# Routing two token blocks at a time, one step of the float64 conversion as a product on ScalarE, and one attention bias table with the local keys first

## Chip, cores and metric

One NeuronCore of a Trainium2 chip runs the whole program. The metric is the device time of one execution in microseconds (us), as the median of several runs. The engines are TensorE (PE in the profile; PEld is its weight load), VectorE (DVE), ScalarE (ACT), GpSimd (POOL) and SyncE (SP), which issues all DMAs.

## What is computed

Windowed attention, then a dense layer with a softmax-times-itself activation and layer norm, then soft routing to 32 slots of 8 experts. Cut to what matters:

```python
# attention: B=4, H=8, S=768, D=64; 8 global keys, 96 local ones; ALiBi bias
scores = q @ k.T / sqrt(D) - slopes * dist           # where (global or local), else -1e9
attn_out = softmax(scores) @ v                       # -> x: 3072 tokens x 512
# dense layer (w_in, w_out, g_ln come as float64)
h = x @ w_in                                         # 512 -> 1024
solu = h * softmax(h)
x = (layer_norm(solu) * g_ln) @ w_out                # 1024 -> 512
# routing
logits = x @ phi                                     # 32 slots
slot_input = softmax(logits, over tokens).T @ x
slot_out = relu(slot_input @ w1[e]) @ w2[e]          # per expert, 32 MB of weights
out = softmax(logits, over slots) @ slot_out
```

## The kernel before

The 3072 tokens are 24 blocks of 128. `fast` (line 949) writes the work down block by block: for block t `att_quad` twice (four heads each, line 569), `x_out`, and seven blocks later `later(u)` (line 931), which is `moe(u)` (dense layer, line 654) and `slots_of(u)` (line 735). Nothing is issued in that order: every instruction is first noted by `Plan`, which gives it a time, dependences and a priority (the table `AHEAD` by stage, and `STAY`, a penalty for a change of the array's shape on TensorE) and from these makes one order for all five engines (`order`, line 273), issued at line 297. So nearly every row of the profile has line 297, and groups are told apart by operation, shape and buffers. In these names `b` is a PSUM bank, `s` one of 25 SBUF slots, `small` statistics, `l` the routing logits of a block, `d` their exponentials by token, `w` the 1024x32 routing weights (w_out times phi), `sel` a 0/1 matrix that sums four row groups, `acc` the running slot input, `c_all` the weights by slot.

The stages overlap, in this order. **Start**: the bias tables (`window_tables`, line 441) and the conversion of the float64 weights in 16 pieces of 128x512 (`from_f64`, line 492) beside the first attention blocks. Without a float64 unit a piece is converted in integers: ScalarE scales the low word (line 502), VectorE cuts out and shifts the exponent and the high mantissa in four instructions (503 to 506), GpSimd adds both (508); for w_in ScalarE then rounds and GpSimd makes the remainder (515, 516).

```python
502  nc.scalar.mul(out=r, in_=lo.bitcast(U32), mul=2.0 ** -29)
503  v.tensor_scalar(out=e, in0=hi, scalar1=0x7FFFFFFF, scalar2=None, op0=ALU.bitwise_and)
504  v.tensor_scalar(out=f32v(e), in0=f32v(e), scalar1=2.0 ** -15, scalar2=None, op0=ALU.max)
505  v.tensor_scalar(out=e, in0=e, scalar1=3, scalar2=0x3FFFFFF8, op0=ALU.logical_shift_left, op1=ALU.bitwise_and)
506  v.scalar_tensor_tensor(out=a, in0=hi, scalar=-0x40000000, in1=e, op0=ALU.bitwise_and, op1=ALU.bitwise_or)
```

**Middle**: attention, dense layer and routing of all blocks, interleaved. TensorE uses its array in four shapes (rows by columns): 128x128 for the dense layer, transposes and the sums with `sel`; 64x128 for scores; 128x64 for probabilities times v; 128x32, four side by side, for `w` times the transposed block (writes 32x128) and for `d` times the block (32x256). `slots_of(u)` transposes the block z into `zt`, multiplies by `w`, copies the logits to `l`, sums them with `sel` by slot and by token, takes maxima on VectorE, exponentials on ScalarE, transposes back, copies to `d`, multiplies with z and adds to `acc`. The banks, `l` and `d` are one set, so blocks follow each other.

**End**: the last block's chain, then the expert weights (`in_wx_dram`, 32 loads of 1 MB on SP's queue, in a slot as soon as it is free), and the output.

Of the kernel before, what the change touches and what calls it, by code (L numbers as in the profile page):

```python
# [19 lines left out]
P = 128  # L20
# [37 lines left out]
class Plan:  # L58
# [10 lines left out]
    TURN, STAY, DEEP = 68, 1405, 240  # L69
    WRITES = ("out", "accum_out")  # L70
    AHEAD = {"att": -306, "conv": -240509, "ct": -76279, "down0": 1160935, "down1": 247683, "init": -225381, "load": -1194339, "logits": -93870, "moe": -2182, "out0": 754080, "out1": 854704, "slots": -134, "sums": -1633483, "tab": 1280994, "tail": -566822, "up": -455794, "w": -331203, "w2": -130175}
# [57 lines left out]
    def time(self, eng, method, args):  # L129
# [10 lines left out]
        if eng == "ACT":  # L140
            more = 93 * hasattr(args.get("bias"), "tensor") + 105 * ("accum_out" in args)
            return (52 if psum else 94) + n * 0.833 + more
        if method == "tensor_tensor":
            return 70 + n * (2.5 if self.cols(args["in1"]) == 512 else 1.87)
# [128 lines left out]
    def order(self, rounds=6, look=102):  # L273
# [46 lines left out]
class Build:  # L320


    def __init__(self, tc, nc, a, out, mem):
# [8 lines left out]
        self.rt_st = Ring(st[:, 104 + 4 * i:108 + 4 * i] for i in range(3))  # L332
# [108 lines left out]
    def window_tables(self):  # L441


        self.stage("tab", 0)
        nc = self.nc
        n = WIN + NGMAX
        win, first = self.tabs[False], self.tabs[True]
        rel, key, keep, nd, past, near = (self.part(S_ZX, n * i, n) for i in range(6))
        ri, ki = (self.part(S_ZX, n * (6 + i), n).bitcast(I32) for i in range(2))
        big = int(BIGF)  # L450
        for tl, o, m, step, base, ch in (
            (ri, 0, PREV, -1, PREV, 1), (ri, PREV, NGMAX, 0, big, 0), (ri, WIN - P, P, -1, 0, 1), (ri, WIN, NGMAX, -1, 0, 1),
            (ki, 0, PREV, 0, big, 0), (ki, PREV, NGMAX, 1, 0, 0), (ki, WIN - P, P, 0, big, 0), (ki, WIN, NGMAX, 1, 0, 0),
        ):
            nc.gpsimd.iota(tl[:, o:o + m], pattern=[[step, m]], base=base, channel_multiplier=ch)
# [36 lines left out]
    def from_f64(self, name, rows, cols, out):  # L492


        nc, v, g = self.nc, self.nc.vector, self.nc.gpsimd
# [73 lines left out]
    def att_quad(self, t, hq):  # L569
# [4 lines left out]
        o, n = (WIN - P, P) if first else (0, WIN)  # L574
        m = WIN - P
# [16 lines left out]
        for i2 in range(2):  # L592
            q = i2 * QK
            with self.together():
                for i, (a, b) in enumerate(parts):
                    for j in range(2):
                        r = slice(64 * j, 64 * j + 64)
                        nc.tensor.matmul(out=ps[j][:, 256 * i2:256 * i2 + n], lhsT=a[r, q:q + P], rhs=b[r, q + P + o:q + QK],
                                         start=(i == 0), stop=(i == len(parts) - 1))
        for h in range(4):  # L600
            i2, j = divmod(h, 2)
            nc.vector.tensor_tensor_reduce(
                out=pr[:, h, o:], in0=ps[j][:, 256 * i2:256 * i2 + n], in1=self.tabs[first][:, 4 * hq + h, :], scale=-0.125,
                scalar=3.0e38, op0=ALU.add, op1=ALU.min, accum_out=st[:, h:h + 1],
            )
        for h in range(4):
            nc.scalar.activation(out=pr[:, h, o:], in_=pr[:, h, o:], func=AF.Exp, bias=st[:, h:h + 1], scale=-1.0,
# [5 lines left out]
        for i2 in range(2):  # L613
            w = pr[:, 2 * i2:2 * i2 + 2]
            nc.gpsimd.tensor_tensor(out=w[:, :, o:], in0=w[:, :, o:],
                                    in1=share[:, 2 * i2:2 * i2 + 2].unsqueeze(2).to_broadcast([P, 2, WIN - o]), op=ALU.mult)
# [3 lines left out]
            with self.together():  # L620
                for j in range(2):
                    nc.tensor.transpose(pt[:, j, :], w[:, j, m:], self.ident)
                if not first:
                    for j in range(2):
                        nc.tensor.transpose(pt[0:m, 2 + j, :], w[:, j, 0:m], self.ident)
# [84 lines left out]
    def last_logits(self, shift, scale):  # L710
# [16 lines left out]
        l4 = self.l4_ring()[0]  # L727
# [7 lines left out]
    def slots_of(self, u):  # L735
        self.stage("slots", u)
        nc = self.nc
        z = self.z.pop(u)
        if u == self.last:
            l4, dT, d = self.l4_ring()  # L740
            by_slot, by_token, pd = self.bank(ZT)[:, 0:P], l4[:, 0:NS], self.bank(LD)
            nc.tensor.transpose(by_slot, l4, self.ident)
        else:
            zt = self.zt_ring().rearrange("p (c n) -> p c n", c=8)
            for half in range(2):
                ps = self.bank(ZT)
                with self.together():
                    for c in range(4):
                        o = (half * 4 + c) * P
                        nc.tensor.transpose(ps[:, c * P:(c + 1) * P], z[:, o:o + P], self.ident)  # L750
                nc.scalar.copy(out=zt[:, half * 4:half * 4 + 4, :], in_=ps.rearrange("p (c n) -> p c n", c=4))
            pl = pd = self.ld_bank(u)
# [463 lines left out]
```

## Time and profile before

| | us |
|---|---|
| runs of before | 442.66, 442.77, 444.25 (median 442.77) |
| the profiled execution, whole | 441.79 |
| its span, first to last instruction | 439.9 |
| TensorE busy | 404.5 (92%) |
| VectorE, ScalarE, GpSimd busy | 335.4, 304.1, 189.2 |
| mean granted TensorE clock | 0.987 |

The span and the 1.9 us around it make the profiled execution's 441.79. TensorE is busy over nine tenths of the span, but the share is an average over stages with different limits, so the stages are read one by one below.

### The profile page before, as it was taken

Reading aid. Unit: us, or ns where it says so; the run is one execution under the profiler, and the core shown is the slowest. Engines: PE = TensorE matmul, PEld = TensorE weight load, DVE = VectorE, ACT = ScalarE, POOL = GpSimd, SP = SyncE. Lnnn points to the kernel's source line nnn. Section 1 sums busy time; section 2 is a strip of 40 time slices with the busy share of each in tenths; the row PEclk is TensorE's granted clock in tenths of the full one; section 3 lists DMA queues with packets and bytes.
Section 4 is the critical chain, followed back from the end, with each engine's and each line's share of the span. In section 5 each row is a group of like instructions: output and inputs, shape, how many; then the busy total and the mean of one; then the engine's idle time right before and its main releaser. Section 6 shows DMA issues by size and latency. Waiting matters only on the chain.

```text
span 439.9 us, 10437 instructions
## 1 busy us (share of the span) xinstructions
PE 404.5 (92%) x3617; PEld 294.4 (67%) x3617; DVE 335.4 (76%) x1337; ACT 304.1 (69%) x973; POOL 189.2 (43%) x181
## 2 busy tenths in 40 slices
PE   2898978999999999999999999999999999899960
PEld 1465655787777887877878778778777776424540
DVE  7878898999997889887778777888768799401370
ACT  4789888876688888988898778988646546411240
POOL 1488887666345365755465465555100003300000
PEclk9999999999999999999999999999999999999995
DMA  7957574636130413233124213202702599899597
GB/s 285 320 199 252 179 250 169 237 99 227 78 115 17 180 35 115 94 116 113 44 79 163 82 74 115 92 2 98 288 20 92 190 369 373 326 397 419 223 338 229
DMA packets 20140, 78.02 MB, mean 177 GB/s; under 512 B 2480, under 2 KB 8624, under 8 KB 15984
## 3 DMA queue, kind: packets, MB, share of 16 engines
q1 hardware_dynamic: 20080, 77.28, 48.7%
q8 instruction: 30, 0.49, 0.5%
q14 instruction: 30, 0.25, 0.2%
HBM read 70.98 MB, written 6.29 MB: 176 GB/s over the span
## 4 chain that ended last, share of the span: by engine, by line
PE 75%; POOL 8%; DVE 6%; ACT 3%; issue 2%; DMA 2%; POOLq 0%; DVEq 0%; ACTq 0%
PE b L297 75%; POOL s L297 8%; ACT s L297 3%; DVE s L297 3%; DVE small L297 2%; DMA out_dram<-s 1%; DMA small<-in_n_dram 1%; DVE acc L297 0%; DVE l L297 0%; ACT l L297 0%; ACT c_all L297 0%; DVE d L297 0%; POOLq L297 0%; DVE sel L297 0%; DVE c_all L297 0%
## 5 line engine op out<-in xcount | busy, mean ns | idle before, releaser
L297 PE MATMUL b<-s,s 128*128 128x512 f32 (+3 forms) x1568 | 235.3, 348 | 6.5 <-ACT s L297 2.8
L297 PEld LDWEIGHTS b<-s,s 128*128 128x128 f32 (+3 forms) x1568 | 150.0, 153 | 52.5 <-issue 14.6
L297 ACT COPY s<-b 128x256 f32<-128x256 f32 (+2 forms) x244 | 95.1, 436 | 46.2 <-PE b L297 44.5
L297 ACT ACTIVATE s<-s,small 128x240 f32<-128x240 f32 (+2 forms) x215 | 117.3, 552 | 10.8 <-DVE small L297 10.8
L297 POOL TENSOR_TENSOR s<-s,small 128x480 f32<-128x480 f32 (+1 forms) x96 | 92.4, 982 | 73.4 <-DVE small L297 50.8
L297 POOL TENSOR_TENSOR s<-s,s 128x736 fp32r<-128x736 f32 (+2 forms) x56 | 89.6, 1603 | 55.1 <-DVE s L297 19.4
L297 PE MATMUL b<-ident,s 128*128 128x128 f32 (+1 forms) x600 | 92.1, 280 | 3.4 <-ACT s L297 2.0
L297 PEld LDWEIGHTS b<-ident,s 128*128 128x128 f32 (+1 forms) x600 | 68.9, 141 | 27.1 <-issue 10.3
L297 DVE CUSTOM_DVE_ANT_0 s<-b,s 128x240 f32<-128x240 f32 (+1 forms) x192 | 65.3, 379 | 6.5 <-PE b L297 5.6
L297 DVE TENSOR_SCALAR small<-small 128x1 f32<-128x1 f32 (+1 forms) x322 | 61.5, 216 | 7.0 <-ACT s L297 2.9
L297 PE MATMUL b<-s 64*128 64x240 f32 (+2 forms) x528 | 52.4, 322 | 9.5 <-DMA s<-in_qkv_dram 6.6
L297 PEld LDWEIGHTS b<-s 64*128 64x128 f32 (+1 forms) x528 | 39.0, 195 | 22.4 <-issue 7.7
L297 DVE TENSOR_REDUCE small<-b 128x1 f32<-128x128 f32 (+2 forms) x95 | 42.3, 463 | 11.9 <-PE b L297 9.3
L297 ACT ACTIVATE s<-b,small 128x512 f32<-128x512 f32 x49 | 33.5, 690 | 16.6 <-DVE small L297 15.2
L297 ACT ACTIVATION_READ_ACCUMULATOR s<-s,small 128x1 f32 x215 | 42.4, 197 | 0.0
L297 DVE SCALAR_TENSOR_TENSOR s<-b,s 128x512 f32<-128x512 f32 x48 | 31.9, 686 | 3.8 <-ACT s L297 3.5
L297 DVE TENSOR_SCALAR s<-s 128x512 int32<-128x512 int32 (+2 forms) x51 | 32.3, 665 | 2.6 <-ACT s L297 2.5
L297 DVE COPY s<-b 128x512 f32<-128x512 f32 (+1 forms) x20 | 12.3, 635 | 23.6 <-PE b L297 22.9
L297 POOL CAST s<-c_all 128x256 fp32r<-128x256 f32 x6 | 2.4, 396 | 60.1 <-DVE s L297 53.6
L297 ACT CAST s<-b 128x512 fp32r<-128x512 f32 (+1 forms) x32 | 18.3, 570 | 14.3 <-PE b L297 14.3
L297 DVE TENSOR_SCALAR s<-s,small 128x1024 f32<-128x1024 f32 (+1 forms) x25 | 23.8, 951 | 0.3
L297 ACT CAST s<-s 128x736 fp32r<-128x736 f32 (+2 forms) x26 | 18.6, 720 | 5.3 <-PE b L297 2.5
(86 smaller groups left out, 315.8 us busy)
## 6 DMA issues: line engine op xcount, KB each, us to landing
s<-in_wx_dram SPq DMA_DIRECT2D x32, 1024.0 KB, 7.8
s<-in_qkv_dram SPq DMA_DIRECT2D x24, 992.0 KB, 4.9
out_dram<-s SPq DMA_DIRECT2D x12, 512.0 KB, 5.5
s<-in_v_tail_dram SPq DMA_DIRECT2D x20, 224.0 KB, 5.6
s<-in_w_in_dram SPq DMA_DIRECT2D x8, 512.0 KB, 6.7
s<-in_w_out_dram SPq DMA_DIRECT2D x8, 512.0 KB, 3.8
acc<-in_phi_dram SPq DMA_DIRECT2D x1, 64.0 KB, 10.2
small<-in_n_dram SPq DMA_DIRECT2D x1, 2.0 KB, 2.7
```

The lines of the kernel that those rows point to most:

```text
L297: f(*(self.now(x, age) for x in a), **{k: self.now(x, age) for k, x in kw.items()})
```

## The change

Four things, and a new order. (1) `later` calls `slots_of(u - 1, u)` after every odd block up to 21; blocks 22 and 23 go alone. For a pair the sum by slot is one matmul of 256 columns, the logits copy, the maxima, the exponentials by slot, the copy to `d` and the update of `acc` are done once, the exponentials by token twice; the eight `d` matmuls follow each other and add up in PSUM. `l` and `d` share one buffer; `zt` has two, the second in slot S_TAB + 1. (2) In `from_f64` ScalarE multiplies the high word, read as a float, by 2^-112; VectorE keeps a shift and the merge. (3) One bias table of 256 columns per head, with the keys of the block itself first, serves first and other blocks. The host lays out keys and values to match, so the same number of DMAs loads them. (4) The planner's numbers (`AHEAD`, `STAY`, `look`, two costs) are others. What is computed is the same.

```diff
-    TURN, STAY, DEEP = 68, 1405, 240
+    TURN, STAY, DEEP = 68, 1362, 240
...
-    AHEAD = {"att": -306, "conv": -240509, "ct": -76279, ...
+    AHEAD = {"att": -720, "conv": -1209974, "ct": 295072, ...
...
-        for hp in range(4):
-            for h in (2 * hp, 2 * hp + 1):
-                for dst, o, m in ((win, 0, WIN), (first, WIN, NGMAX)):
-                    nc.vector.scalar_tensor_tensor(
-                        out=dst[:, h, 0:m], in0=nd[:, o:o + m], scalar=8.0 * SLOPES[h], in1=keep[:, o:o + m],
-                        op0=ALU.mult, op1=ALU.add,
-                    )
-            hs = slice(2 * hp, 2 * hp + 2)
-            nc.scalar.copy(out=first[:, hs, NGMAX:], in_=win[:, hs, WIN - P + NGMAX:])
+        for h in range(H):
+            nc.vector.scalar_tensor_tensor(out=self.table[:, h, :], in0=nd, scalar=8.0 * SLOPES[h], in1=keep, op0=ALU.mult,
+                                           op1=ALU.add)
...
         nc.scalar.mul(out=r, in_=lo.bitcast(U32), mul=2.0 ** -29)
-        v.tensor_scalar(out=e, in0=hi, scalar1=0x7FFFFFFF, scalar2=None, op0=ALU.bitwise_and)
-        v.tensor_scalar(out=f32v(e), in0=f32v(e), scalar1=2.0 ** -15, scalar2=None, op0=ALU.max)
-        v.tensor_scalar(out=e, in0=e, scalar1=3, scalar2=0x3FFFFFF8, op0=ALU.logical_shift_left, op1=ALU.bitwise_and)
-        v.scalar_tensor_tensor(out=a, in0=hi, scalar=-0x40000000, in1=e, op0=ALU.bitwise_and, op1=ALU.bitwise_or)
+        nc.scalar.mul(out=f32v(e), in_=f32v(hi), mul=2.0 ** -112)
+        v.tensor_scalar(out=e, in0=e, scalar1=3, scalar2=None, op0=ALU.logical_shift_left)
+        v.scalar_tensor_tensor(out=a, in0=hi, scalar=-0x80000000, in1=e, op0=ALU.bitwise_and, op1=ALU.bitwise_or)
...
+            nc.vector.tensor_copy(out=l4, in_=pl[:, 0:k * P])
...
+                nc.tensor.matmul(out=by_slot, lhsT=self.sel4, rhs=l4, start=True, stop=True)
+                for i in range(k):
+                    nc.tensor.matmul(out=by_token[:, i, :], lhsT=l4[:, i * P:(i + 1) * P], rhs=self.sel4[:, 0:32], start=True,
+                                     stop=True)
...
+        nc.vector.tensor_copy(out=d, in_=pd[:, 256:256 + k * P].rearrange("p (k n) -> p k n", k=k)[:, :, 0:NS])
+        with self.together():
+            for i, z in enumerate(zs):
+                for fq in range(4):
+                    nc.tensor.matmul(out=pd[32 * fq:32 * fq + 32, 0:256], lhsT=d[:, i, :], rhs=z[:, fq * 256:(fq + 1) * 256],
+                                     start=(i == 0), stop=(i == k - 1), tile_position=(0, 32 * fq))
...
         self.moe(u)
-        self.slots_of(u)
+        if u == self.last - 1 or u == self.last:
+            self.slots_of(u)
+        elif u % 2:
+            self.slots_of(u - 1, u)
...
-        self.zt_ring = Ring([self.part(S_ZX, 1024, 1024)])
+        self.zt_ring = Ring([self.part(S_ZX, 1024, 1024), self.part(S_TAB + 1, 0, 1024)])
```

Three places show how the order moves. First, TensorE in the middle: `b_68` is the routing bank, `b_61` to `b_67` the others, `w_72` or `w_71` the routing weights. Before, the four `d` matmuls of one block and the eight `w` matmuls of a later one:

```order
L297 MATMUL b_68<-s_100,d 32x256 x4
L297 MATMUL b_66<-s_96,s_92 128x512
L297 MATMUL b_65<-s_94,s_92 128x512
L297 MATMUL b_66<-s_94,s_92 128x512
L297 MATMUL b_63<-ident,s_84 128x128 x2
L297 MATMUL b_63<-ident,s_84 112x128 x2
L297 MATMUL b_67<-ident,s_84 128x128 x2
L297 MATMUL b_67<-ident,s_84 112x128 x2
L297 MATMUL b_68<-s_101,w_72 32x128 x8
```

Now, those of two pairs:

```order
L297 MATMUL b_67<-ident,s_98 128x128 x4
L297 MATMUL b_68<-s_99,l_69 32x256 x8
L297 MATMUL b_64<-s_1118,s_87 64x128 x2
L297 MATMUL b_64<-s_1118,s_84 64x128 x2
L297 MATMUL b_67<-ident,s_98 128x128 x4
L297 MATMUL b_66<-s_93,s_91 128x512
L297 MATMUL b_68<-s_82,w_71 32x128 x8
L297 MATMUL b_68<-s_100,w_71 32x128 x8
```

Eight `d` and sixteen `w` matmuls now stand together, so the shape 128x32 is entered half as often for them.

Second, ScalarE at the start. `s_103`, `s_104` are conversion buffers before and `s_101` to `s_103` now, with `s_104`, `s_105` the raw float64 data; `s_84` or `s_83` hold attention probabilities. Before:

```order
L297 CAST s_101<-s_101 128x256 x2
L297 COPY s_83<-s_82 128x2x112 x3
L297 ACTIVATE s_84,small<-s_84,small 128x128 x4
L297 COPY s_83<-s_82 128x2x112
L297 ACTIVATE s_103<-s_105 128x512
L297 ACTIVATE s_84,small<-s_84,small 128x128 x4
L297 ACTIVATE s_104<-s_105 128x512
```

Now:

```order
L297 CAST s_100<-s_100 128x256 x2
L297 ACTIVATE s_101<-s_104 128x512
L297 ACTIVATE s_102<-s_104 128x512
L297 ACTIVATE s_101<-s_104 128x512
L297 ACTIVATE s_103<-s_104 128x512
L297 ACTIVATE s_83,small<-s_83,small 128x128 x4
L297 ACTIVATE s_102<-s_105 128x512
L297 ACTIVATE s_103<-s_105 128x512
```

Two pieces of the conversion now come ahead of the first exponentials, and the four table copies are gone. On SP's queue the first two pieces of w_in now stand ahead of the first block's `in_qkv_dram` load, which was first.

Third, VectorE after the last block's dense layer, whose bn_stats and bn_aggr mark the place (`s_100` or `s_99` is the last z). Before:

```order
L297 SCALAR_TENSOR_TENSOR s_100,small<-b_61,s_101 128x512
L297 COPY d<-b_68 128x32
L297 COPY l_69<-b_63 128x128
L297 SCALAR_TENSOR_TENSOR s_100,small<-b_62,s_101 128x512
L297 SCALAR_TENSOR_TENSOR acc<-acc,small,b_68 128x256
L297 BN_STATS small<-s_100 128x6
L297 TENSOR_REDUCE small<-b_63 128x1
L297 TENSOR_REDUCE small<-small 128x2
L297 TENSOR_SCALAR small<-small 128x1 x2
L297 BN_STATS small<-s_100 128x6
L297 TENSOR_SCALAR small<-small 128x1
L297 BN_AGGR small<-small 128x2
```

Now:

```order
L297 SCALAR_TENSOR_TENSOR acc<-acc,small,b_68 128x256
L297 SCALAR_TENSOR_TENSOR s_99,small<-b_61,s_100 128x512
L297 SCALAR_TENSOR_TENSOR s_99,small<-b_62,s_100 128x512
L297 BN_STATS small<-s_99 128x6
L297 COPY l_69<-b_68 128x128
L297 BN_STATS small<-s_99 128x6
L297 TENSOR_REDUCE small<-small 128x2
L297 TENSOR_SCALAR small<-small 128x1 x2
L297 TENSOR_REDUCE small<-b_68 128x1
L297 TENSOR_SCALAR small<-small 128x1
L297 BN_AGGR small<-small 128x2
```

Blocks 20 and 21 are now done as one ahead of this place, so fewer routing instructions of earlier blocks stand between those of the last block.

## Rows read from the trace of the kernel before

**Rows 1.** Windows by stage: us; then busy us (instructions) of each engine; clock, DMA.

```profile
20.00:77.00 57.00, 49.51 (x401) 31.88 (x401) 49.01 (x166) 49.54 (x167) 47.48 (x42) 1.00 0.62 211
77.00:364.00 287.00, 286.81 (x2550) 224.87 (x2547) 242.30 (x1012) 222.40 (x716) 129.34 (x107) 1.00 0.34 122
364.00:379.00 15.00, 13.32 (x137) 8.59 (x135) 13.66 (x61) 9.05 (x32) 5.57 (x10) 1.00 0.94 380
```

**Rows 2.** Timeline of PE in the middle: start, us, operation, count.

```profile
203.87 0.64 PE L297 MATMUL b<-s,d 128*32 128x256 f32 x8
204.44 0.73 PE L297 MATMUL b<-s,s 128*128 128x512 f32 x2
205.01 1.04 PE L297 MATMUL b<-ident,s 128*128 128x128 f32 x8
205.98 0.94 PE L297 MATMUL b<-s 64*128 64x240 f32 x12
206.85 0.66 PE L297 MATMUL b<-ident,s 128*128 128x128 f32 x4
207.43 0.32 PE L297 MATMUL b<-s,w 128*32 128x128 f32 x4
```

**Rows 3.** Timeline of PE in windows of 0.01 to 0.05 us, for single starts.

```profile
205.45 0.49 PE L297 MATMUL b<-ident,s 128*128 128x128 f32 x3
...
204.78 0.39 PE L297 MATMUL b<-s,s 128*128 128x512 f32 x1
...
200.30 0.63 PE L297 MATMUL b<-s,s 128*128 128x512 f32 x2
...
200.53 0.63 PE L297 MATMUL b<-s,s 128*128 128x512 f32 x2
```

**Rows 4.** Groups by line and form, 20 to 77 us: count, busy us, mean ns, idle before.

```profile
L297 DVE TENSOR_SCALAR s<-s 128x512 int32<-128x512 int32 x16 | 13.5, 853 | 0.0
...
L297 DVE TENSOR_SCALAR s<-s 128x512 f32<-128x512 f32 x8 | 6.3, 783 | 0.0
L297 ACT ACTIVATE s<-s 128x512 int32<-128x512 uint32 x9 | 6.1, 682 | 0.3 <-POOL s L297 0.3
```

**Rows 5.** Timeline of DVE and POOL near 18 us, and of DVE near 23 us.

```profile
18.07 1.27 POOL L297 TENSOR_TENSOR s<-s,s 128x512 int32<-128x512 int32 x1 [2.56 <-DVE s L297]
...
18.11 1.52 DVE L297 TENSOR_SCALAR s<-s 128x512 int32<-128x512 int32 x1
...
22.93 0.42 DVE L297 TENSOR_SCALAR s<-s 128x512 int32<-128x512 int32 x1
```

**Rows 6.** Groups by line and form, whole span.

```profile
L297 DVE SCALAR_TENSOR_TENSOR acc<-acc,small,b 128x256 f32<-128x256 f32 x23 | 11.0, 476 | 4.3 <-PE b L297 4.0
...
L297 DVE COPY l<-b 128x128 f32<-128x128 f32 x24 | 6.9, 287 | 6.1 <-PE b L297 5.8
L297 DVE TENSOR_REDUCE small<-b 128x1 f32<-128x128 f32 x24 | 6.9, 286 | 3.6 <-PE b L297 3.3
...
L297 DVE COPY d<-b 128x32 f32<-128x32 f32 x24 | 4.6, 190 | 4.9 <-PE b L297 4.6
...
L297 DVE TENSOR_REDUCE small<-b 128x1 f32<-128x32 f32 x23 | 4.3, 187 | 1.8 <-ACT l L297 1.6
...
L297 ACT COPY s<-s 128x224 f32<-128x224 f32 x4 | 1.5, 374 | 5.6 <-DVE s L297 5.6
```

**Rows 7.** Chain that ended last, 365.8 to 378.2 us: shares, then pieces (start, us).

```profile
by line: DVE small L297 48.3%; DVE acc L297 14.5%; DVE s L297 11.7%; PE b L297 8.2%; ACT s L297 5.5%; DVE l L297 4.3%; DVE d L297 3.8%; ACT l L297 3.6%; issue 3.0%; DVE c_all L297 2.2%; DVEq L297 0.6%
...
368.09 2.38 DVE small L297 x12
...
377.56 0.40 DVE acc L297
```

**Rows 8.** Waits of the whole span: who for whom, us, times, longest.

```profile
PE b L297 <- DMA s<-in_qkv_dram: 6.6, 1, 6.6
...
PEld b L297 <- DMA s<-in_wx_dram: 0.3, 1, 0.3
```

More of the change, by code (lines that the diff above doesn't have):

```diff
@@ L271, in schedule, with order @@
         return start, fin, nth
-    def order(self, rounds=6, look=102):
+    def order(self, rounds=6, look=121):
         n = len(self.ops)
@@ L331, in __init__ @@
         self.ln_st = Ring(st[:, 48 + 14 * i:62 + 14 * i] for i in range(4))
-        self.rt_st = Ring(st[:, 104 + 4 * i:108 + 4 * i] for i in range(3))
+        self.rt_st = Ring(st[:, 104 + 6 * i:110 + 6 * i] for i in range(2))
         self.rs_st = Ring(st[:, 116 + 2 * i:118 + 2 * i] for i in range(4))
@@ L573, in att_quad @@
         first = t % NQB == 0
-        o, n = (WIN - P, P) if first else (0, WIN)
-        m = WIN - P
+        n, m = P if first else WIN, WIN - P
         x = self.qkv[t]
@@ L597, in att_quad @@
                         r = slice(64 * j, 64 * j + 64)
-                        nc.tensor.matmul(out=ps[j][:, 256 * i2:256 * i2 + n], lhsT=a[r, q:q + P], rhs=b[r, q + P + o:q + QK],
+                        nc.tensor.matmul(out=ps[j][:, 256 * i2:256 * i2 + n], lhsT=a[r, q:q + P], rhs=b[r, q + P:q + P + n],
                                          start=(i == 0), stop=(i == len(parts) - 1))
@@ L602, in att_quad @@
             nc.vector.tensor_tensor_reduce(
-                out=pr[:, h, o:], in0=ps[j][:, 256 * i2:256 * i2 + n], in1=self.tabs[first][:, 4 * hq + h, :], scale=-0.125,
+                out=pr[:, h, 0:n], in0=ps[j][:, 256 * i2:256 * i2 + n], in1=self.tabs[first][:, 4 * hq + h, :], scale=-0.125,
                 scalar=3.0e38, op0=ALU.add, op1=ALU.min, accum_out=st[:, h:h + 1],
@@ L732, in last_logits, with slots_of @@
         )
-    def slots_of(self, u):
-        self.stage("slots", u)
+    def slots_of(self, *us):
+        self.stage("slots", us[0])
         nc = self.nc
[L738 to L741, printed above, removed]
+        k = len(us)
+        zs = [self.z.pop(u) for u in us]
+        l4_all = self.l4_ring()
+        l4, dT = (l4_all[:, 0:P], l4_all[:, P:]) if us[0] == self.last else [l4_all[:, 0:k * P]] * 2
+        d = l4_all[:, 0:k * NS].rearrange("p (k s) -> p k s", k=k)
+        if us[0] == self.last:
+            pd, by_slot, by_token = self.bank(LD), self.bank(ZT)[:, 0:P], l4[:, 0:NS].unsqueeze(1)
@@ L752, in slots_of @@
-            pl = pd = self.ld_bank(u)
-            by_slot, by_token = pl[:, 128:256], pl[:, 256:288]
-            with self.together():
-                for r in range(2):
-                    for g in range(4):
-                        nc.tensor.matmul(out=pl[32 * g:32 * g + 32, 0:P], lhsT=self.w2[:, r * 4 + g, :],
-                                         rhs=zt[:, r * 4 + g, :], start=(r == 0), stop=(r == 1), tile_position=(0, 32 * g))
-            l4, dT, d = self.l4_ring()
-            nc.vector.tensor_copy(out=l4, in_=pl[:, 0:P])
@@ L761, in slots_of @@
-            nc.tensor.matmul(out=by_slot, lhsT=self.sel4, rhs=l4, start=True, stop=True)
-            nc.tensor.matmul(out=by_token, lhsT=l4, rhs=self.sel4[:, 0:32], start=True, stop=True)
+            pl = pd = self.ld_bank(us[0])
+            by_slot, by_token = pl[:, 256:256 + k * P], pl[:, 0:k * NS].rearrange("p (k s) -> p k s", k=k)
+            for i, z in enumerate(zs):
+                zt = self.zt_ring().rearrange("p (c n) -> p c n", c=8)
+                for half in range(2):
+                    ps = self.bank(ZT)
+                    with self.together():
+                        for c in range(4):
+                            o = (half * 4 + c) * P
+                            nc.tensor.transpose(ps[:, c * P:(c + 1) * P], z[:, o:o + P], self.ident)
+                    nc.scalar.copy(out=zt[:, half * 4:half * 4 + 4, :], in_=ps.rearrange("p (c n) -> p c n", c=4))
+                with self.together():
+                    for r in range(2):
+                        for g in range(4):
+                            nc.tensor.matmul(out=pl[32 * g:32 * g + 32, i * P:(i + 1) * P], lhsT=self.w2[:, r * 4 + g, :],
+                                             rhs=zt[:, r * 4 + g, :], start=(r == 0), stop=(r == 1), tile_position=(0, 32 * g))
@@ L951, in fast @@
         S = self.slots
-        self.tabs = {
-            False: self.part(S_TAB, 0, H * WIN).rearrange("p (h n) -> p h n", h=H),
-            True: self.part(S_TAB + 1, 0, H * P).rearrange("p (h n) -> p h n", h=H),
-        }
+        self.table = self.part(S_TAB, 0, H * (WIN + NGMAX)).rearrange("p (h n) -> p h n", h=H)
+        self.tabs = {False: self.table[:, :, NGMAX:], True: self.table[:, :, 0:P]}
         self.pt_ring = Ring(self.part(S_TAB + 1, 1024 + 512 * i, 512) for i in range(2))
```

74 lines of the change are left out of this document (35 added, 39 removed).

## Prediction

> **What bounds the kernel now.** The windows by stage come first [rows 1], since the busy share of the whole span mixes stages. In the middle, from 77 to 364 us, TensorE is busy 286.81 of 287.00 us; VectorE has 242.30, ScalarE 222.40 and GpSimd 129.34, so all three have room. There only what shortens TensorE's own stream counts. In the start, from 20 to 77 us, four engines are busy 47.5 to 49.5 of 57 us: none is the bound, each waits for another, and TensorE loses 57.00 - 49.51 = 7.5 us. From 364 to 379 us VectorE is busiest, 13.66 of 15.00, and the chain that ended last [rows 7] names it at each step: 48.3 + 14.5 + 11.7 + 4.3 + 3.8 + 2.2 = 85% of the stretch is VectorE's, in small instructions of 2.38 / 12 = 0.2 us. After 379 us come the expert weights, for which TensorE waits 0.3 us in all [rows 8]; the change has nothing there.
>
> The other view is the timeline of TensorE inside the middle [rows 2, 3], for the price of a change of array shape. Four transposes follow each other from 205.01 to 205.45 us, 0.11 us each. The run of eight that starts at 205.01 is entered without a change and left with one: 205.98 - 205.01 = 0.97 = 8 x 0.11 + 0.09. The run of four at 206.85 is entered and left with one: 0.58 = 4 x 0.11 + 0.14. So leaving a shape costs 0.09 us and the first weights of the next one 0.05 more. For the dense layer the step is 200.53 - 200.30 = 0.23, and after a change 204.78 - 204.44 = 0.34, so 0.11 more. A change costs 0.09 to 0.20 us.
>
> **The change, part by part.**
>
> *TensorE in the middle.* Its instructions are the same but for eleven sums by slot, which are twice as wide instead of two; the columns that stream are the same, so I count nothing there. At the most, if a double one cost no more than a single, it would give 11 x 2 passes x 0.11 = 2.4 us. What moves is the sequence. I counted in both orders how often consecutive matmuls have another array shape, from the place that TensorE reaches at 77 us to the last matmul of the dense layer: 161 times before, 127 now. Of the 34 that go, 18 lead into 128x32 and 14 back into 128x128, which is what pairs should do; for scores and values it is three fewer and one more. The price is between 34 x 0.09 = 3.1 and 34 x 0.20 = 6.8 us. I take 0.145 us, the middle, since half lead into a shape with few weights to load: **4.9 us off**. Nothing covers them, as TensorE is never idle there.
>
> *VectorE and ScalarE in the middle.* Pairs take work from both, and the rest of the conversion adds a few multiplications to ScalarE. Both have over 40 us of room in the stage [rows 1], so this counts as nothing; if the room went, TensorE would stall for what is missing.
>
> *The pair's wait.* Block u - 1 now waits for u before its routing, and z, `l` and `d` are held longer. Behind the wait stand the next `d` matmuls on TensorE, and the dense layer two blocks on, which needs the buffer of z. The order puts some 40 to 70 rows of other matmuls between a pair's `w` and `d` runs, which at 0.1 us and more each are several us, so I count nothing; the other end is a stall of the length of one maximum and one copy, 0.29 + 0.19 us [rows 6], at each of eleven pairs: 5.3 us lost. A gain is excluded, since TensorE loses nothing there now.
>
> *The conversion.* Per piece VectorE loses two of its three tensor_scalar instructions, at 853 and 783 ns between 20 and 77 us [rows 4]: eight pieces fall in the stage, 8 x (0.85 + 0.78) = 13 us of its 49. ScalarE gains one multiplication per piece, by its nearest row the 682 ns of the low word, 16 x 0.68 = 10.9 us. Up to the first exponential of the dense layer the order has 23 such instructions on ScalarE instead of 12, so 11 x 0.68 = 7.5 us more, less the four table copies at 374 ns [rows 6], so 6.0 us on an engine that has 57.0 - 49.5 = 7.5 us free. Most it can give: the 7.5 us that TensorE loses there. Most it can cost: 6.0 us at the density that ScalarE has reached, 49.54 / 57 = 0.87, so 6.9 us. I take **nothing**, since VectorE's relief and ScalarE's load are of one size and four conversions move ahead of the first exponentials, into time in which ScalarE had little.
>
> [...]
>
> *The first block.* Its load now stands behind two half-size pieces of w_in. TensorE waited 6.6 us for it [rows 8] and VectorE's tables were later still, so of the roughly 3 us of delay about 1 us is seen, and ScalarE uses the time. This lies inside the bounds of the start.
>
> *The tables.* Eight instructions of 256 columns instead of eight of 240 and eight of 16, and no copies: counted with the conversion. The other layout of keys and values moves no work.
>
> *The last blocks.* Between the last block's maximum and the last update of `acc`, the order of VectorE loses two updates of `acc`, one maximum by slot, two by token, two copies to `d`, one to `l` and five small instructions. By rows 6 and the 0.2 us of rows 7: 2 x 0.476 + 0.286 + 2 x 0.187 + 2 x 0.190 + 0.287 + 5 x 0.2 = 3.3 us of a chain that is VectorE's to 85%. At most 3.3, at least nothing, if ScalarE's exponentials and TensorE's transposes of the last block, which remain, come next. I take **2.0 us off**.
>
> *Expert weights.* Slot S_TAB + 1 holds `zt` until block 22, so its load goes from ninth to fourteenth in the last batch, and five loads stand behind it. With a wait of 0.3 us in 32 loads [rows 8] I count nothing.
>
> **Sum.** Against the profiled execution: 441.79 - 4.9 - 2.0 = 434.9 us. The median of the runs stands 442.77 - 441.79 = 1.0 us above that execution, so **435.9 us**. Its own range takes 3.1 and 6.8 for the shapes, 0 and 3.3 for the end, and some 2 us either way in the start: 431 to 442.
>
> **Rivals**, as medians.
>
> 1. *ScalarE becomes the bound of the start.* Its multiplications stand in one queue with the exponentials and the copies on which GpSimd and TensorE wait. For it: 6.0 us into 7.5 us of room. Against it: the work moved ahead. Price up to 6.9 us: 442.8, no change. Chance 0.14.
> 2. *It is the bound beyond the start too: slower.* All sixteen multiplications, less the copies, at that density: (10.9 - 1.5) / 0.87 = 10.8 us on TensorE's path, 435.9 + 10.8 = 446.7. It decides once the start loses over 6.9 + 2.2 us. Against it: between 77 and 364 us ScalarE is busy 77% of the time. Chance 0.08.
> 3. *The start gains.* A tensor_scalar of VectorE that began with a GpSimd addition took 1.52 us instead of 0.42 [rows 5]; with most of them gone both engines wait less, and TensorE gets up to 7.5 us back: about 5, so 430.9. [...] Against it: ScalarE's load stays. Chance 0.15.
> 4. *Pairs stall TensorE*, as bounded above: 441.2. Against it: the distance in the order. Chance 0.05.
>
> My forecast has 0.58.
>
> **How the numbers follow.** About 0.5% of this kernel's time, 2.2 us, can be told from no change. Faster by more than that, under 440.6: the forecast and the third rival, 0.73. Within it: the first and the fourth, with 0.19, less a little that goes slower: 0.18. Slower: 0.09. The range reaches from the third rival's 430 to just past the first's, 443.5, and leaves out the second and the far end of the third.
>
> **What would show it.** Right: the stretch in which TensorE is never idle is some 5 us shorter with the same matmuls, and the last chain of VectorE, 12.4 us long in rows 7, is near 10. The start shows ScalarE above 90% and VectorE below 75%, and TensorE is saturated again near 77 us. Wrong: saturated only after 82 us (the first two rivals), before 73 (the third), or waits of TensorE for `l` at the `d` matmuls in the middle (the fourth). If the shapes were counted right and priced wrong, the middle shrinks by another amount with no idle time.

## The result, and the profile after

The changed kernel takes **436.05 us** (median of four, 434.6 to 436.36) against 442.73 (442.66 to 444.25) for the kernel before in the same comparison: a ratio of 0.9835, 95% interval 0.9804 to 0.9865. The forecast was 435.9. The profiled execution took 434.6 us, with a span of 432.9; the sum of the prediction for it was 434.9.

In both kernels an execution's time goes with its mean granted clock (the changed kernel took 434.6 us at 0.987 and 436.04 to 436.36 at 0.983 to 0.985, the kernel before 441.79 at 0.987 and, over all comparisons below, 442.3 to 443.2 at 0.982 to 0.986), so where medians stand at different clocks executions of like clock are compared too ("at like clock"), and the medians of "old numbers" and "order with 170" leave out three executions at 0.970 or less.

To compare both programs at the same place in the work, take the start of the last dense-layer matmul (362.85 us before, 356.52 after) and the first transpose of `acc` (378.00 and 370.67). The windows by stage, for the kernel before:

```profile
0.00:20.00 20.00, 9.97 (x47) 6.47 (x48) 15.52 (x70) 11.23 (x37) 5.71 (x21) 1.00 0.90 309
...
77.00:362.85 285.85, 285.66 (x2541) 223.86 (x2538) 241.27 (x1010) 222.40 (x716) 129.34 (x107) 1.00 0.34 120
362.85:378.00 15.15, 13.51 (x140) 8.97 (x138) 14.17 (x61) 8.72 (x32) 4.67 (x9) 1.00 0.96 387
```

and for the changed kernel (its second row answers to the first of [rows 1]):

```profile
0.00:20.00 20.00, 8.38 (x40) 5.50 (x42) 15.34 (x56) 12.32 (x37) 8.68 (x22) 1.00 0.88 331
20.00:77.00 57.00, 52.23 (x413) 34.31 (x411) 47.73 (x162) 54.64 (x178) 46.55 (x41) 1.00 0.66 230
77.00:356.52 279.52, 279.48 (x2550) 224.75 (x2550) 230.65 (x912) 222.12 (x693) 125.60 (x105) 1.00 0.32 116
356.52:370.67 14.15, 11.85 (x112) 7.63 (x110) 12.59 (x49) 8.32 (x27) 6.20 (x12) 1.00 0.95 360
```

The span is 439.9 - 432.9 = 7.0 us shorter, and four differences add up to it:

- TensorE's busy time up to the last dense-layer matmul: before 9.97 + 49.51 [rows 1] + 285.66 = 345.14, after 8.38 + 52.23 + 279.48 = 340.09, so **5.05 us less**. The place is the same for the dense layer, but not for the routing: up to it the trace has 3000 matmuls now and 2986 before (among them sixteen more of `w` and eight more of `d`), some 2 us of work, estimated from the steps of the timeline. For the same work the fall is larger; over the whole span TensorE's busy time went from 404.5 to 396.7 us, 7.8 less.
- Its idle time up to there: 362.85 - 345.14 = 17.71 and 356.52 - 340.09 = 16.43, **1.28 less**.
- From there to the transpose of `acc`: 15.15 and 14.15, **1.0 less**.
- From the transpose to the end of the span: 61.9 and 62.2, 0.3 more.

In the middle TensorE is busy 279.48 of 279.52 us, so nothing of the pairs makes it wait. In the start ScalarE is busy 54.64 of 57 us. VectorE, however, did not become free. Groups by form, 20 to 77 us, of the changed kernel, against [rows 4]:

```profile
L297 POOL TENSOR_TENSOR s<-s,s 128x512 int32<-128x512 int32 x10 | 14.1, 1415 | 2.0 <-ACT s L297 2.0
L297 DVE SCALAR_TENSOR_TENSOR s<-s,s 128x512 int32<-128x512 int32 x11 | 11.9, 1082 | 0.2
...
L297 DVE TENSOR_SCALAR s<-s 128x512 int32<-128x512 int32 x10 | 8.7, 880 | 0.1
```

The tensor_scalar instructions that went are gone (x10 here, x16 and x8 in rows 4), but more pieces fall into the stage (11 merges, 9 before), and the merge of the two parts, with two inputs, takes 1.08 us in the mean. VectorE's busy time fell from 49.01 to 47.73 us only.

The same merge took 0.81 us in the mean over the whole run of the kernel before and 1.03 now. Where GpSimd runs nothing at the same time a merge takes 0.68 to 0.69 us in both kernels; 8 of 16 lay beside a GpSimd instruction before and took 0.68 to 1.67 us, 0.93 in the mean, and 11 of 16 do now, with 0.66 to 1.60 us and a mean of 1.19.

The chain that ended last in the final stretch of the changed kernel, 356.5 to 370.7 us, shares by line and the longest pieces:

```profile
by line: DVE small L297 42.0%; DVE s L297 22.4%; PE b L297 20.6%; DVE acc L297 6.1%; DVE l L297 5.2%; ACT s L297 4.2%; issue 3.6%; DVEq L297 0.1%
...
357.60 1.70 PE b L297 x20
...
359.81 1.22 DVE s L297 x4
365.91 1.14 DVE s L297
```

It is still VectorE's, to some three quarters (42.0 + 22.4 + 6.1 + 5.2%), but near its start stands a piece of 1.70 us of TensorE: twenty matmuls, sixteen of them the pair's `d`, ahead of the pair's update of `acc`.

### The profile page after: what moved, and what is told of

It reads as the page before. It is cut to its first block, busy times and chain, and to the rows that moved or that the text cites. A ratio compares the mean times of both kernels' runs of the same rounds, so it can differ in the third digit from the quotient of the medians.

```text
span 432.9 us, 10268 instructions
## 1 busy us (share of the span) xinstructions
PE 396.7 (92%) x3595; PEld 294.8 (68%) x3595; DVE 321.6 (74%) x1209; ACT 308.8 (71%) x952; POOL 187.5 (43%) x180
## 4 chain that ended last, share of the span: by engine, by line
PE 80%; ACT 6%; DVE 6%; POOL 2%; DMA 2%; issue 1%; SPq 0%; DVEq 0%; POOLq 0%; ACTq 0%
PE b L297 80%; ACT s L297 6%; DVE s L297 3%; DVE small L297 2%; POOL s L297 2%; DMA s<-in_qkv_dram 2%; DVE l L297 1%; SPq L297 0%; DVE acc L297 0%; DVE small L383 0%; DVE small L381 0%; DVE small L382 0%; DVE small L384 0%; DVE small L379 0%; DVEq L297 0%
## 5 line engine op out<-in xcount | busy, mean ns | idle before, releaser
L297 PEld LDWEIGHTS b<-s,s 128*128 128x128 f32 (+3 forms) x1568 | 149.4, 153 | 42.9 <-issue 11.1
L297 ACT COPY s<-b 128x256 f32<-128x256 f32 (+1 forms) x244 | 94.9, 438 | 36.2 <-PE b L297 34.6
L297 POOL TENSOR_TENSOR s<-s,s 128x736 fp32r<-128x736 f32 (+2 forms) x56 | 90.2, 1615 | 61.9 <-ACT s L297 30.5
L297 POOL TENSOR_TENSOR s<-s,small 128x480 f32<-128x480 f32 (+1 forms) x96 | 89.7, 954 | 60.6 <-DVE small L297 39.3
L297 PE MATMUL b<-ident,s 128*128 128x128 f32 (+1 forms) x600 | 90.8, 279 | 5.6 <-ACT s L297 3.2
L297 DVE TENSOR_SCALAR small<-small 128x1 f32<-128x1 f32 (+2 forms) x289 | 60.1, 215 | 13.4 <-ACT s L297 6.0
L297 PE MATMUL b<-s 64*128 64x240 f32 (+2 forms) x528 | 52.1, 320 | 11.1 <-DMA s<-in_qkv_dram 9.3
L297 DVE TENSOR_REDUCE small<-b 128x1 f32<-128x512 f32 (+3 forms) x73 | 39.0, 557 | 7.1 <-PE b L297 5.7
L297 PE MATMUL b<-s,l 128*32 128x256 f32 (+1 forms) x320 | 27.4, 469 | 1.2 <-DVE l L297 0.9
L297 DVE TENSOR_REDUCE small<-small 128x4 f32<-128x8 f32 (+2 forms) x96 | 14.8, 154 | 13.4 <-ACT s L297 12.1
L297 ACT ACTIVATE s<-s 128x512 f32<-128x512 f32 (+1 forms) x32 | 21.3, 691 | 2.8 <-DMA s<-in_w_in_dram 2.8
```

What stands on the lines that cost most here:

```text
L297: f(*(self.now(x, age) for x in a), **{k: self.now(x, age) for k, x in kw.items()})
```

## The experiments

Each run is timed beside the kernel before, and its ratio is to that. TensorE's busy and idle time up to the last dense-layer matmul are worked out as above, from the windows of the profiled execution; changes of array shape are counted in the order of the program up to the same place.

| kernel | median us | ratio, 95% interval | last dense matmul | busy | idle | changes |
|---|---|---|---|---|---|---|
| before | 442.73 | | 362.85 | 345.14 | 17.71 | 222 |
| changed | 436.05 | 0.9835, 0.9804-0.9865 | 356.52 | 340.09 | 16.43 | 187 |
| `d` groups split | 439.75 | 0.9925, 0.9897-0.9954 | 361.23 | 343.65 | 17.58 | 205 |
| pair groups split | 443.21 | 1.001, 0.9992-1.0028 | 362.56 | 345.72 | 16.84 | 207 |
| no pairs | 447.42 | 1.0124, 1.0083-1.0164 | 369.00 | 347.94 | 21.06 | 228 |
| old numbers | 449.6 | 1.0147, 1.0124-1.017 | 366.01 | 344.07 | 21.94 | 208 |
| before, new conversion | 447.0 | 1.0113, 1.0088-1.0138 | 365.75 | 344.98 | 20.77 | 215 |
| old conversion | 446.29 | 1.007, 1.0039-1.0101 | 368.89 | 347.34 | 21.55 | 199 |
| no product | 432.93 | 0.9768, 0.974-0.9795 | 354.81 | 339.25 | 15.56 | 187 |
| product on VectorE | 441.77 | 0.9955, 0.9933-0.9977 | 361.54 | 343.12 | 18.42 | 187 |
| first load first | 437.54 | 0.987, 0.9842-0.9897 | 358.86 | 340.10 | 18.76 | 187 |
| 20 and 21 alone | 436.45 | 0.9861, 0.9843-0.9879 | 356.95 | 340.88 | 16.07 | 187 |
| middle reordered | 434.46 | 0.9816, 0.9789-0.9843 | 356.13 | 339.71 | 16.42 | 184 |
| order with 170 | 439.09 | 0.9919, 0.9895-0.9943 | 361.30 | 341.32 | 19.98 | 170 |

### The price of a change of shape

**`d` groups split.** A step behind the planner holds back half of a group:

```diff
+        yield op["calls"][:4] if one else op["calls"]
+        if one:
+            late = i
+        elif late is not None and op["eng"] == "PE" and op["passes"][0][0] == (128, 128):
+            yield ops[late]["calls"][4:]
```

> The changed kernel with one thing more: in nine pairs, up to block 17, the second four of the eight d matmuls are put behind the next transposes or dense-layer matmul. Nothing but the update of acc waits for them, and that is not urgent; the end of the program is as changed. TensorE's array changes shape 18 times more, all of it where TensorE is never idle. Theory (a change costs 0.145 us, and the 34 fewer were the gain): 18 x 0.145 = 2.6 above 436.05, so 438.7, with 437.7 to 439.7 for prices of 0.09 to 0.20. Rival (the earlier splitting of w groups, 7.1 us for 20 changes, shows the real price, 0.35 us): 442.4. Rival (shapes are free, the waits cost): 436.0.

It took 439.75, 3.7 more and just above the range; at like clock (439.46 to 439.82 at 0.988 to 0.990) it is 5 us. TensorE's timeline at one of the nine places shows the price itself. The changed kernel:

```profile
151.85 1.07 PE L297 MATMUL b<-s,l 128*32 128x256 f32 x16
152.86 1.98 PE L297 MATMUL b<-s,s 128*64 128x128 f32 x32
154.77 0.44 PE L297 MATMUL b<-ident,s 128*128 128x128 f32 x2
154.96 1.17 PE L297 MATMUL b<-s,s 128*128 128x512 f32 x4
```

and with the group split:

```profile
152.25 0.64 PE L297 MATMUL b<-s,l 128*32 128x256 f32 x8
152.82 1.98 PE L297 MATMUL b<-s,s 128*64 128x128 f32 x32
154.73 0.44 PE L297 MATMUL b<-ident,s 128*128 128x128 f32 x2
155.10 0.64 PE L297 MATMUL b<-s,l 128*32 128x256 f32 x8
155.67 0.98 PE L297 MATMUL b<-s,s 128*128 128x512 f32 x3
```

The sixteen passes went from 1.01 us (152.86 - 151.85) to 0.57 + 0.57 = 1.14, and the two transposes from 0.19 (154.96 - 154.77) to 0.37: together 0.13 + 0.18 = 0.31 us for two changes, 0.155 each, against the 0.145 of the prediction. Read in the same way, the nine places give 0.28 to 0.36 us for two changes, 2.8 in all. The other 1.9 of the 4.71 us by which the last dense-layer matmul is later come between the places: 1.08 us of them are idle time after 77 us (284.23 - 283.11 in the window 77 to 361.23, against 0.04 as changed), the rest the profile counts as busy. So the price stands in place, and the whole run paid nearly twice as much for the same changes.

**Pair groups split**, the blunter form run first, moves whole groups of eight out of ten pairs, two changes each:

```diff
-        return sorted(range(n), key=lambda i: (start[i], nth[i]))
+        return spread(self.ops, pred, sorted(range(n), key=lambda i: (start[i], nth[i])))
```

> The changed kernel with one thing more: in ten of the pairs the second group of eight w (or d) matmuls is taken out of its run and put behind the dense-layer matmul or the transposes that follow it. The instructions are the same, nothing else moves, and TensorE's array changes shape 20 times more, all of it where TensorE is never idle. Theory (the gain of the change is the 34 changes fewer, at 0.145 us each): 20 x 0.145 = 2.9 us above the changed kernel's 436.05, so 439.0, with 1.8 to 4.0 us for prices of 0.09 to 0.20; the stretch in which TensorE is never idle grows by just that. Rival (the changes of shape are hidden, the gain is VectorE's and ScalarE's fewer instructions): no change, 436.0.

It took 443.21, far over the range. Up to 341 us of the profiled execution nine moves, 18 changes, had added 3.5 us to TensorE's timeline, 0.2 per change. The logits copies waited with the `w` groups, and from 77 us to the last dense-layer matmul TensorE was idle for 285.56 - 284.97 = 0.59 us, against 0.04 as changed. The tenth move put the second group of the last pair, next to the end, 3 us further back, and from 365 to 368 us TensorE's clock was granted at 0.55, 0.50 and 0.50. As a price of the shape this run is too dirty; as an answer to the rival, that shapes are hidden, it is clear enough.

**No pairs.**

```diff
-        elif u % 2:
-            self.slots_of(u - 1, u)
+        else:
+            self.slots_of(u)
```

> The changed kernel with every block routed alone; conversion, tables and the planner's numbers stay as changed. The order then has 228 changes of shape up to the last dense-layer matmul (187 as changed, 222 before). Theory: 41 x 0.145 = 5.9 us for the shapes, 0.6 for the eleven double sums by slot, and the 1.0 us that the end was seen to lose: 7.5 above 436.05, so 443.6, with 441 to 445. Rival (the planner's new numbers made the gain): 436 to 438. Rival (the conversion made it): 436 to 438.

447.42, outside on the slow side: busy time is 7.85 us up for 41 changes, where the theory had 5.9 + 0.6 = 6.5 (the 0.6 an estimate that no timeline bears out) and the clock was at 0.50 from 35 to 38 us, and idle time, which the expectation left out, is 4.6 up. Neither rival's time came. But the numbers stayed those of the program with pairs, so the run doesn't show what they or the conversion would give in an order made for single blocks.

**Old numbers.**

```diff
-    TURN, STAY, DEEP = 68, 1362, 240
+    TURN, STAY, DEEP = 68, 1405, 240
```

with `AHEAD` and `look` of before.

> The program as changed, ordered with the planner's numbers of before (AHEAD, STAY, look): 208 changes of shape up to the last dense-layer matmul instead of 187. Theory: 21 x 0.145 = 3.0 above 436.05, so 439.1, with 438 to 441, the idle time of the start apart. Rival (the new numbers carry the change and the parts do nothing by themselves): 442.7 or more. Rival (the numbers do nothing): 436.

449.6. Busy time is 3.98 us up for 21 changes, but idle time 5.5, and the stretch from the last dense-layer matmul to the transpose of `acc` takes 19.73 us instead of 14.15, with the clock at 0.50 to 0.68 from 371 to 375. The numbers of one program lose time on the other, and this run can't tell "the numbers carry the change" from "these numbers don't fit". It does show that the 35 changes fewer are not the pairs' alone: with the old numbers pairs take the count from 222 to 208 only, and with the new ones from 228 to 187.

Over most rows of the table busy time goes with the count of changes: 339.7 at 184, 339.3 to 340.9 at 187, 343.7 at 205, 344.1 at 208, 345.0 at 215, 345.1 at 222, a slope of 0.14 to 0.2 us per change (with some work shifted past the place in the last two, as said above). Four rows lie above that line and had the clock at 0.50 for some microseconds before 95 us: old conversion, product on VectorE, no pairs, pair groups split. The order with 170 changes lies above it at full clock, so the count isn't all that sets busy time.

### The conversion and the start

**New conversion alone**, in the kernel before with its own numbers (the three lines of `from_f64` in the diff above).

> The kernel before with the new conversion alone (one product on ScalarE, one shift and the merge on VectorE); its planner's numbers stay. The order has 215 changes of shape up to the last dense-layer matmul instead of 222. Theory (the conversion is worth nothing by itself): 442.7 less 7 x 0.145 = 1.0, so 441.7, with 440 to 443. Rival (the start gains, since VectorE waits less for GpSimd): 437.7. Rival (ScalarE becomes the bound of the start): 446 or more.

447.0, slower, where no gain and no loss were expected. Busy time hardly moved, idle time rose by 3.1 us: the planner now put the first block's load so late that the first matmul came at 11.4 us. The time is that of the second rival, but its mechanism is not what the trace shows: between 20 and 77 us, where ScalarE was to bind, TensorE idles 57.00 - 51.41 = 5.6 us against 7.5 before. The theory missed, since it took the order as given.

**Old conversion** in the changed kernel, ordered anew.

> The changed kernel with the old conversion (three shifts and masks and the merge on VectorE, one product on ScalarE). The order has 199 changes of shape up to the last dense-layer matmul instead of 187. Theory: 436.05 + 12 x 0.145 = 437.8, and up to 1.1 more, which is what TensorE's idle time in the first 77 us fell by: 437.8 to 438.9. Rival (the conversion made the gain): 441 or more. Rival (ScalarE's sixteen products cost time, which the pairs paid for): 433 to 435.

446.29 (443.0 to 448.96), beyond what the theory allowed and in the range of the first rival. It has 5.1 us more idle time, and in the profiled execution, the slowest of seven, TensorE's clock was at 0.50 from 75 to 88 us:

```profile
77.00:100.00 23.00, 21.71 (x116) 16.65 (x116) 19.16 (x38) 11.56 (x26) 8.47 (x7) 0.75 0.45 148
```

The execution at 0.989 took 443.0, so the clock is not all of it. Both runs let the planner order the program anew, and so mix the conversion with the order; neither shows that the conversion made the gain. The next two hold the order and exchange the product alone.

**No product.**

```diff
-        nc.scalar.mul(out=f32v(e), in_=f32v(hi), mul=2.0 ** -112)
-        v.tensor_scalar(out=e, in0=e, scalar1=3, scalar2=None, op0=ALU.logical_shift_left)
-        v.scalar_tensor_tensor(out=a, in0=hi, scalar=-0x80000000, in1=e, op0=ALU.bitwise_and, op1=ALU.bitwise_or)
+        v.tensor_scalar(out=e, in0=hi, scalar1=3, scalar2=0x3FFFFFF8, op0=ALU.logical_shift_left, op1=ALU.bitwise_and)
+        v.scalar_tensor_tensor(out=a, in0=hi, scalar=-0x40000000, in1=e, op0=ALU.bitwise_and, op1=ALU.bitwise_or)
```

> The changed kernel in its own order, without the product of the conversion on ScalarE: the shift on VectorE reads the high word itself and masks it, which leaves out the treatment of weights beyond single precision's range. VectorE keeps two instructions per piece, ScalarE loses sixteen of 0.69 us, 11.1 us in all, nearly all of them before 77 us. Theory as predicted (ScalarE's load in the start lies beside other work): 436.0, down to 435. Rival (ScalarE, busy 54.64 of 57 us there, is what the start waits for): TensorE gets back most of the 6.8 us that it idles between its first matmul and 77 us: 430 to 432.

432.93, between theory and rival: the products cost 3.1 us by the medians, but these stand at different clocks; at like clock it is 434.6 - 432.9 = 1.7 us, of 11.1 us of ScalarE's work. It is the fastest kernel here, but it does less.

**Product on VectorE**, at the same place in the order.

```diff
-        nc.scalar.mul(out=f32v(e), in_=f32v(hi), mul=2.0 ** -112)
+        v.tensor_scalar(out=f32v(e), in0=f32v(hi), scalar1=2.0 ** -112, scalar2=None, op0=ALU.mult)
```

> The changed kernel in its own order, with the sixteen products issued on VectorE at the same places in the order. ScalarE loses 11.1 us, VectorE gains sixteen tensor_scalar instructions at 0.85 us beside GpSimd's additions, 13.6 us, of which some ten, 8.5 us, lie between 20 and 77 us, where VectorE is busy 47.73 of 57 us. Theory (the move to ScalarE was right because GpSimd holds VectorE up): VectorE reaches 56 of 57 us, TensorE loses 2 to 5 us: 438 to 441. Rival (VectorE undisturbed needs 0.42 us for each, and ScalarE is the fuller engine): 16 x (0.69 - 0.42) = 4.3 us gained: 432 to 434.

441.77, 5.7 more than with the product on ScalarE, and 4.7 at like clock (439.33 at 0.988). The direction and the rough size of the theory hold, though the time is just above its range and VectorE reached 52.40 of 57 us, not 56. Groups by form, 20 to 77 us:

```profile
L297 DVE TENSOR_SCALAR s<-s 128x512 int32<-128x512 int32 x9 | 8.9, 984 | 0.0
L297 DVE TENSOR_SCALAR s<-s 128x512 f32<-128x512 f32 x9 | 7.3, 816 | 0.0
L297 ACT ACTIVATE s<-s 128x512 int32<-128x512 uint32 x9 | 6.0, 675 | 0.0
```

The product takes 0.82 us on VectorE there; on ScalarE the sixteen took 11.1 us, 0.69 each.

The rival reckoned with 0.42 us, which a tensor_scalar of this size took in the kernel before where GpSimd ran nothing (at 50.41 and 74.65 us of its span), and by that this run should have gained. Beside a GpSimd that is busy 45.92 of the 57 us VectorE does not get it.

**First load first.**

```diff
+    head = [i for i in order if ops[i]["stage"] == ("load", 0)]
+    return head + [i for i in order if i not in head]
```

> The changed kernel in its own order, but with the first block's load put first on SP's queue, ahead of the two pieces of w_in, as it was before. The first matmul comes at 6.6 us again instead of 9.3. Theory as predicted (of the delay about 1 us was seen): 435.0, with 434.5 to 436. Rival (the pieces of w_in come 2.7 us later, and VectorE, ScalarE and GpSimd are late for the whole start): 437 to 439.

437.54: the rival. The first matmul starts at 5.61 us instead of 9.34, and then TensorE waits. Waits of 0 to 40 us, this run:

```profile
PE b L297 <- DVE small L297: 7.8, 2, 6.9
...
ACT s L297 <- DMA s<-in_w_in_dram: 5.2, 1, 5.2
```

The second wait was 2.8 us in the changed kernel. The later load, which the prediction booked as a delay, is a gain in this order: 1.5 us by the medians, 2.3 at like clock (436.84 to 437.0 at 0.987 to 0.989).

### The end, and other orders

**Blocks 20 and 21 alone.**

```diff
-        if u == self.last - 1 or u == self.last:
+        if u >= self.last - 3:
```

> The changed kernel with blocks 20 and 21 routed alone, so that no pair is left in the last stretch; the order has 187 changes of shape up to the last dense-layer matmul, as many as the changed kernel. Theory (the pair takes VectorE work out of the end): from the start of the last dense-layer matmul to the first transpose of acc 15.1 us as before instead of 14.1, so 437.0, up to 438 with one more update of acc ahead of it. Rival (the eight d matmuls of the pair, for whose end the update of acc waits 0.8 us, cost the end as much as the pair saves): 435 to 436.

The stretch takes 15.49 us (356.95 to 372.44) instead of 14.15, so the pair is worth 1.3 us there, as the theory has it. The time of 436.45 lies between theory and rival: the medians differ by 0.4 only, since all four executions here stand at 0.988, and at like clock it is 436.25 to 436.95 against 434.6. The updates of `acc` show both sides, groups of the stretch, first this run, then the changed kernel:

```profile
L297 DVE SCALAR_TENSOR_TENSOR acc<-acc,small,b 128x256 f32<-128x256 f32 x4 | 1.9, 474 | 0.3 <-PE b L297 0.3
L297 DVE TENSOR_SCALAR s<-s,small 128x1024 f32<-128x1024 f32 x2 | 1.6, 807 | 0.0
```

```profile
L297 DVE TENSOR_SCALAR s<-s,small 128x1024 f32<-128x1024 f32 x2 | 2.0, 986 | 0.0
L297 DVE SCALAR_TENSOR_TENSOR acc<-acc,small,b 128x256 f32<-128x256 f32 x3 | 1.4, 474 | 0.8 <-PE b L297 0.8
```

**An order with 170 changes**, found by a search over the planner's order of all engines, whose list takes the place of the order:

```diff
-        return sorted(range(n), key=lambda i: (start[i], nth[i]))
+        return ORDER
```

> The changed kernel, instruction for instruction, in another order that a search over the planner's order found with the number of shape changes in its aim: 170 up to the last dense-layer matmul instead of 187. Theory (each costs 0.145 us where TensorE is never idle): 17 x 0.145 = 2.5 below 436.05, so 433.6, with 432 to 435. Rival (a run of TensorE that waits for its neighbour of the same shape makes others late, as the waits after the split d groups did): 436 to 438.

439.09 (ratio 0.9919, 0.9895 to 0.9943), slower than even the rival had it. The windows up to the last dense-layer matmul, of the execution of 445.91 us, whose clock is full up to there:

```profile
0.00:20.00 20.00, 8.04 (x38) 5.40 (x40) 14.59 (x56) 12.13 (x36) 8.39 (x21) 1.00 0.87 327
20.00:77.00 57.00, 49.67 (x383) 34.58 (x382) 41.77 (x143) 49.87 (x164) 41.85 (x38) 1.00 0.58 201
77.00:361.30 284.30, 283.61 (x2581) 229.86 (x2580) 222.13 (x932) 227.75 (x709) 130.85 (x110) 1.00 0.34 121
```

Of the 17 changes that went, 13 lie before 77 us (49 there now, 62 as changed), where TensorE waits anyway, so the theory's premise, that each goes where TensorE is never idle, held for four. TensorE idles 2.9 us more before 77 us (19.29 against 16.39) and 0.65 more after; its busy time is 1.2 us up in spite of the fewer changes, for a reason that stays open.

**Middle reordered**: the same edit with another list, in which TensorE's order alone is altered, between 78 and 338 us.

> The changed kernel with only TensorE's order between 78 and 338 us altered, by a search in which each move had to hold as well with later operands and slower other engines; the orders of the other engines, the start and the end are as changed. 184 changes of shape up to the last dense-layer matmul instead of 187. Theory (3 x 0.145 = 0.4 us for the shapes and up to 1 us for the end, where the last dense layer gets its operands sooner): 434.6 to 435.6. Rival (what the first search met: an order that pays by the planner's numbers makes TensorE wait on the chip): 437 or more.

434.46, just under the range of the theory. The last dense-layer matmul starts 0.39 us sooner, as the three changes ask (0.4), and the profiled execution is 0.4 us shorter (434.2 and 434.6). The time is below both kernels', but its interval, 0.9789 to 0.9843, overlaps that of the changed kernel: of those that compute the same it is the fastest here, by about what can be told apart or less.

## Why the prediction was right, and where it was not

- **TensorE in the middle, -4.9**: right in cause, and near in size. The split `d` groups give 0.155 us per change in place, the reordered middle 0.13, so 35 changes are worth some 5 us. The 5.05 us by which busy time fell looks like the same number, but is for more work than before; for the same work it is some 2 us more (7.8 over the whole span), and what gave these no run shows. It was not the eleven wide sums by slot: in the timelines a wide pass takes 0.215 us and a narrow one 0.11. Pairs and planner's numbers share the 35.
- **Room of VectorE and ScalarE, the pair's wait, 0 each**: right, TensorE loses 0.04 us in the middle. The fourth rival falls.
- **The conversion, nothing**: the start lost 1.28 us of idle time, so the number was near; the reason was not. "VectorE's relief and ScalarE's load are of one size" failed on VectorE's side: it was to fall below 75% of 20 to 77 us and is at 84% (47.73 of 57). ScalarE above 90% was right (96%). The product is not hidden either: leaving it out gives 1.7 us at like clock. The first two rivals had the mechanism but not the amount; the third, that VectorE and GpSimd get free, did not come.
- **The first block, about 1 us seen**: wrong in sign in this order. Putting the load back first costs 1.5 us, or 2.3 at like clock.
- **The last blocks, -2.0**: half of it came, 1.0. VectorE's busy time from the last dense-layer matmul to the transpose fell by 14.17 - 12.59 = 1.6 us, with three updates of `acc` instead of five. Against that, VectorE waits 0.8 us for the pair's matmuls before one update, and the two scalings of z take 0.99 instead of 0.81 us each, 0.4 us more. The prediction counted what left the chain and not what the pair puts ahead of it. Its sign, a last chain near 10 us instead of 12.4, came by half: from VectorE's first product of the last block to the transpose it is 12.1 us before (from 365.93) and 10.95 now (from 359.72).
- **Expert weights, tables, 0**: from the transpose of `acc` to the end 0.3 us were lost.
- **The sum**: -4.9, 0 and -2.0 were forecast, -5.05, -1.28 and -1.0 came. The total fits (434.9 and 434.6), partly by luck: the misses of start and end cancel.

What the chosen numbers of the planner share in the gain stays open: no run separated the order of the start from the edits in it, and none gave the kernel without pairs numbers chosen for it.

## What to carry to other kernels

Where one engine is never idle, count what its stream contains besides work, here changes of array shape, price one from two neighbouring rows of the timeline, and multiply. That price held in place (0.155 us against 0.145), but only for changes where the engine is never idle, and the whole run with the `d` groups split lost more than it, 4.7 us against 2.8, of which 1.1 us are waits. Where several engines wait for each other, single instructions couldn't be costed by busy shares (ScalarE's products, 11.1 us of its time, cost 1.7 us); hold the order and exchange one instruction to learn its price. An order made by a planner belongs to the program it was made for: after an edit, ordering anew without new numbers lost 4 to 14 us here.

## What the hardware showed that was not expected

TensorE's granted clock fell in some executions and not in others, at the same place of the same order. The kernel with the pair groups split has the same order as the changed kernel up to 113 us, and the same idle time from 32 to 34 us. Windows of the split kernel, then of the changed one:

```profile
32.00:34.00 2.00, 0.86 (x5) 0.55 (x5) 2.00 (x6) 2.00 (x8) 2.00 (x3) 1.00 0.64 211
34.00:38.00 4.00, 3.94 (x22) 2.85 (x23) 2.61 (x6) 3.00 (x9) 4.00 (x4) 0.57 0.27 70
```

```profile
32.00:34.00 2.00, 0.87 (x5) 0.55 (x5) 2.00 (x6) 2.00 (x8) 2.00 (x3) 1.00 0.36 135
34.00:38.00 4.00, 3.83 (x38) 2.65 (x40) 3.93 (x14) 3.83 (x12) 4.00 (x4) 1.00 0.46 141
```

In the first TensorE goes on at 0.50 of full speed (the windows of 34 to 37 us show 0.51, 0.50 and 0.50, the next 0.79), by estimate from the 0.57 for (1 - 0.57) x 4 / 0.50 = 3.4 us, and the work behind is 1.3 us late; the timeline shows the eight scores passes that follow at 1.70 us, against 1.08 in the changed kernel. TensorE had waited 1.2 us for GpSimd just before in both. The clock was at 0.50 after idle time also in the runs without pairs (35 to 38 us, TensorE busy 0.00 from 33 to 34), with the product on VectorE (89 to 92, busy 0.25 and 0.30 in the two microseconds from 85) and, for longest, with the old conversion (75 to 88, busy 0.27 and 0.58 in the two from 72). A stretch like these is the likely reason why the changed kernel's other executions took 436.0 to 436.4 us: their mean clock was 0.983 to 0.985, against 0.987 in the one of 434.6. Where in them the clock was low is not shown, since they left no trace. An idle microsecond of TensorE in the start can so be followed by a loss of more than itself (here 1.2 us and then 1.3), which the prediction's sum had no term for; it isn't shown that the idle time alone decides it.
